# Five empty SyncE instructions behind the issue of SyncE's last store

## The chip, the cores and the metric

One core of a Trainium2 chip. The time is the device time of one execution in microseconds (us).

## The reference

A block of two branches on a 2048 x 640 bf16 input: a layer norm, a spectral filter (2-D real FFT, product with complex weights, inverse FFT) and a gated feed-forward network of width 1536.

```python
xn = _layernorm(x, axis=-1)
s = _A_ref(xn, A_w_r, A_w_i)                       # irfft2(rfft2(xn) * W)
g = _silu(_B_ref(xn, B_w_gate, B_w_up, B_w_down))  # (gelu(xn @ wg) * (xn @ wu)) @ wd
return x + s * g
```

## The kernel before

The kernel describes its work as tasks. A small planner of its own decides on which engine and in which order they run, and then every task emits its instructions. SyncE does nothing but wait and issue DMAs (its 211 records before: 134 issues, 73 semaphore checks, 4 drains); ScalarE issues the last piece of the last output tile.

```python
    def dma(out, in_, rank, size, after=(), new=(), use=(), slow=1.0, land=0):
        return add(lambda e: nc.sync.dma_start(...), "SP", (430, 430), rank, ...)   # cut
    ...
    if last and hi == D:
        add(lambda e: nc.scalar.dma_start(out=outv[:, n1, lo:], in_=res.tile[:, lo:]), "ACT", ...)
        return
    dma(lambda: outv[:, n1, lo:hi], lambda: res.tile[:, lo:hi], (0, 0, n1), ...)
    ...
    with tc.manual_schedule():
        for t in plan.run():
            t.emit(t.on)
    # leaving the tile context adds the closing sequence: SyncE makes nine checks of
    # semaphores, drains, and all five engines meet in a barrier
```

Of the kernel before, what the change touches and what calls it, by code (L numbers as in the profile page):

```python
# [222 lines left out]
def kernel(  # L223
# [11 lines left out]
    nc = tc.nc  # L235
# [778 lines left out]
    with tc.manual_schedule():  # L1014
        for t in plan.run():
            t.emit(t.on)


# [28 lines left out]
```

## Time and profile before

| | before |
|---|---|
| time, median of 3 runs | 202.47 us (202.35 to 202.68) |
| span of the profiled run | 200.7 us |
| TensorE busy | 195.5 us, 97% |
| last matmul to the end of the span | 196.74 to 200.72 us, 3.98 us |
| issue of SyncE's last store to the end | 197.61 to 200.72 us, **3.11 us** |

The last row I call *the stretch*.

L1042 is the closing line of the kernel (columns of its profile lines: engine, operation, count, shortest/median/longest duration in ns, first and last start).

```profile
L1042 SPq DRAIN  x2: 13/64/114, 199.4 to 199.8; - x2
```

Two drains follow one another on SyncE with nothing recorded between them. The first has ended at 199.459 us, the second starts at 199.849 us: a gap of 0.39 us, behind the last landing. I call it *the halt*; a *record* is one instruction as the trace lists it. The chain view does not show it either: its last step ends at 197.72 us, three us ahead of the end of the span.

### The profile page before, as it was taken

The numbers are of one execution on the slowest core, as the hardware profiler recorded it, in microseconds if no ns is written. First come the engines' busy times: TensorE is split into PE (matmuls) and PEld (weight loads), VectorE is DVE, ScalarE is ACT, GpSimd is POOL, SyncE is SP. The second block draws the span as 40 slices with busy tenths as digits, with TensorE's granted clock in tenths as the row PEclk, the third lists the DMA queues.
The fourth block names the chain that finished last, engine by engine and source line by source line (L and its number), as shares of the span: only waits on it lengthen the run. The fifth ranks groups of instructions, "written<-read, shape, count | busy, mean of one in ns | idle before, by whom it ended". The sixth has DMA issues, their size and how long they took to land.

```text
span 200.7 us, 4126 instructions
## 1 busy us (share of the span) xinstructions
PE 195.5 (97%) x1527; PEld 118.2 (59%) x1527; DVE 148.6 (74%) x318; ACT 128.3 (64%) x226; POOL 32.8 (16%) x71
## 2 busy tenths in 40 slices
PE   7999999999999999999999999999999999999992
PEld 3994444667544655777755455467765555457781
DVE  3689999996524159999998999933157788787773
ACT  3899989763722767767775767233466565776451
POOL 2414333896000000000000000000004122211210
PEclk9999999999999999999999999999999999999999
DMA  6999999896639976333244110116704242332432
GB/s 180 325 316 325 339 393 225 207 257 171 207 76 349 340 179 135 92 97 122 61 118 132 68 65 1 69 64 215 309 3 141 90 134 98 102 104 92 131 103 67
DMA packets 35895, 32.63 MB, mean 163 GB/s; under 512 B 10910, under 2 KB 32930, under 8 KB 35874
## 3 DMA queue, kind: packets, MB, share of 16 engines
q1 hardware_dynamic: 34434, 29.49, 50.4%
q0 software_dynamic: 1152, 2.66, 4.9%
q10 hardware_dynamic: 288, 0.20, 0.5%
q8 instruction: 12, 0.20, 0.4%
q14 instruction: 9, 0.07, 0.1%
HBM read 22.51 MB, written 9.19 MB: 158 GB/s over the span
## 4 chain that ended last, share of the span: by engine, by line
PE 97%; DVE 0%; ACT 0%; issue 0%; DVEq 0%
PE pg L886 26%; PE pu L886 26%; PE pg L976 13%; PE pu L976 13%; PE sp L697 3%; PE sp L830 3%; PE sp L772 2%; PE sp L806 2%; PE sp L368 2%; PE sp L670 2%; PE sp L532 2%; PE sp L690 1%; PE sp L824 1%; PE sp L463 1%; PE sp L478 1%; PE sp L653 0%
## 5 line engine op out<-in xcount | busy, mean ns | idle before, releaser
L886 PE MATMUL pu<-xnT,Wu 128*128 128x512 bf16 (+1 forms) x245 | 57.6, 366 | 0.0
L886 PE MATMUL pg<-xnT,Wg 128*128 128x512 bf16 (+1 forms) x245 | 57.5, 366 | 0.0
L907 DVE TENSOR_TENSOR uT<-pu,ge 128x512 bf16<-128x512 f32 x46 | 31.8, 690 | 20.6 <-PE pu L886 17.5
L976 PEld LDWEIGHTS <-uT 128*128 128x128 bf16 x396 | 37.9, 98 | 13.5
L903 ACT ACTIVATE ge<-pg 128x512 bf16<-128x512 f32 x46 | 27.6, 599 | 24.9 <-PE pg L886 24.4
L886 PEld LDWEIGHTS <-Wg 128*128 128x128 bf16 x285 | 25.5, 99 | 22.1
L886 PEld LDWEIGHTS <-Wu 128*128 128x128 bf16 x285 | 25.0, 98 | 21.6
L976 PE MATMUL pg<-Wd,uT 128*128 128x320 bf16 (+2 forms) x204 | 30.8, 293 | 0.0
L296 ACT CAST ma<-sp 128x644 bf16<-128x644 f32 (+1 forms) x32 | 23.4, 792 | 9.7 <-PE sp L830 7.9
L976 PE MATMUL pu<-Wd,uT 128*128 128x320 bf16 (+1 forms) x192 | 29.3, 297 | 0.0
L932 POOL COPY xr<-s 1x1 bf16<-1x1 bf16 x1 | 0.2, 179 | 100.3 <-DVE s L856 100.3
L933 POOL DMA_DIRECT2D xr<-in_A_x_dram x16 | 8.8, 550 | 32.3 <-DVE res L960 30.2
L296 ACT CAST IU<-sp 128x640 bf16<-128x640 f32 x16 | 10.9, 691 | 4.2 <-PE sp L772 4.1
L296 ACT CAST Vt<-sp 128x640 bf16<-128x640 f32 x16 | 10.8, 691 | 3.7 <-PE sp L806 3.7
L296 ACT CAST mc<-sp 128x640 bf16<-128x640 f32 x16 | 10.8, 700 | 3.4 <-DMA D<-mc 2.8
L985 ACT ACTIVATE th<-pu 128x320 f32<-128x320 f32 x15 | 6.6, 438 | 9.6 <-PE pu L976 9.3
L990 DVE SCALAR_TENSOR_TENSOR G<-th,pg 128x320 bf16<-128x320 f32 x15 | 7.2, 483 | 7.1 <-ACT th L985 6.9
L985 ACT ACTIVATE th<-pg 128x320 f32<-128x320 f32 x15 | 6.7, 445 | 7.8 <-PE pg L976 7.7
L990 DVE SCALAR_TENSOR_TENSOR G<-th,pu 128x320 bf16<-128x320 f32 x15 | 7.3, 484 | 4.6 <-ACT th L985 4.4
L433 POOL TENSOR_TENSOR RSTD<-MVA,mh 128x1 f32<-128x1 f32 x12 | 9.8, 815 | 4.0 <-DVE MVA L415 3.2
L848 DVE TENSOR_TENSOR mb<-ma 128x640 bf16<-128x640 bf16 x8 | 3.9, 491 | 6.8 <-ACT ma L296 6.8
L960 DVE TENSOR_TENSOR res<-yg,xr 128x640 bf16<-128x640 bf16 (+2 forms) x18 | 8.0, 449 | 0.2
(107 smaller groups left out, 255.1 us busy)
## 6 DMA issues: line engine op xcount, KB each, us to landing
BU<-D SPq DMA_DIRECT2D x8, 640.0 KB
D<-mc SPq DMA_DIRECT2D x8, 320.0 KB
D<-IU SPq DMA_DIRECT2D x8, 320.0 KB
xr<-in_A_x_dram POOLq DMA_DIRECT2D x16, 160.0 KB, 2.6
out_dram<-res SPq DMA_DIRECT2D x15, 160.0 KB
Wg<-in_B_w_gate_dram SPq DMA_DIRECT2D x6, 320.0 KB
Wu<-in_B_w_up_dram SPq DMA_DIRECT2D x6, 320.0 KB
Wd<-in_B_w_down_dram SPq DMA_DIRECT2D x6, 320.0 KB
```

The lines of the kernel that those rows point to most:

```text
L296: return nc.scalar.copy(out=out, in_=in_) if e == "ACT" else nc.vector.tensor_copy(out=out, in_=in_)
L433: nc.gpsimd.tensor_tensor(out=rstd, in0=var, in1=mh, op=ALU.pow)
L697: nc.tensor.matmul(into(q, ri), lhsT=sZ.tile[:, q, ri, :], rhs=FM[:, kinds[q][2] + (4 if ri and kind == 0 else 0), :], start=False, stop=T ...
L830: nc.tensor.matmul(into(q, s), lhsT=svs[s].tile[:, c, :], rhs=IM[:, q, :], start=False, stop=True, skip_group_check=True)
L886: nc.tensor.matmul(ps.tile[:, lo:hi + more], lhsT=w[:, c, t * P:(t + 1) * P], rhs=XR[:, c, lo + (lo > 0):hi + 1 if lo or more else hi] if ...
L903: nc.scalar.activation(out=ge.tile, in_=pg.tile if src is None else src, func=ACT.Gelu_apprx_tanh)
L907: nc.vector.tensor_tensor(out=u.tile, in0=pu.tile if src is None else src, in1=ge.tile, op=ALU.mult)
L933: nc.gpsimd.dma_start(out=sx.tile, in_=xv[:, n1, :])
L960: (nc.gpsimd if n1 in () else nc.vector).tensor_tensor(out=res.tile[:, lo:hi], in0=yg.tile[:, lo:hi], in1=sx.tile[:, lo:hi], op=ALU.add)
L976: nc.tensor.matmul(ps.tile[:, 0:hi - lo], lhsT=uT[grp, ks[i]].tile[:, j * P:(j + 1) * P], rhs=Wd[:, ks[i], lo:hi], start=(i == 0), stop=(i ...
L985: nc.scalar.activation(out=th.tile[:, 0:hi - lo], in_=ps.tile[:, 0:hi - lo], func=ACT.Tanh, scale=0.5)
L990: nc.vector.scalar_tensor_tensor(out=G2.tile[:, lo:hi], in0=th.tile[:, 0:hi - lo], scalar=1.0, in1=ps.tile[:, 0:hi - lo], op0=ALU.add, op1 ...
```

## The change

The intent is to place five instructions that do nothing on SyncE, behind its last store, and to keep the compiler from removing them.

```diff
     with tc.manual_schedule():
         for t in plan.run():
             t.emit(t.on)
+        for _ in range(5):
+            nc.sync.nop(nofuse=True)
```

## The prediction

The sum of the forecast is 202.47 + 0 = 202.47 us. The upper end of "all the ways above", 203.0 us, was that third rival: 202.47 us and, as an estimate, the 0.53 us that the last packet of queue q14 took in the trace of before (at 200.46 us).

> **What bounds the kernel now.** I read four views, in this order: the granted clock with the share table, the chain that ended last, the waits of SyncE's queue, and then the closing line of the kernel (the one that every engine shares at the end) cut into narrow windows.
>
> The page says first that the time is matrix time, and the chain says it again:
>
> ```profile
> span 200.7 us, 4126 instructions
> ## 1 busy us (share of the span) xinstructions
> PE 195.5 (97%) x1527; PEld 118.2 (59%) x1527; DVE 148.6 (74%) x318; ACT 128.3 (64%) x226; POOL 32.8 (16%) x71
> ...
> ## 4 chain that ended last, share of the span: by engine, by line
> PE 97%; DVE 0%; ACT 0%; issue 0%; DVEq 0%
> ```
>
> TensorE is busy for 195.5 of 200.7 us, and the chain that ended last is 97% TensorE. SyncE is on no step of it. A change that touches SyncE alone can therefore reach the end only in the few us behind the last matmul, where TensorE has nothing left. (The busy share alone is no proof that the array is at its peak, since matmul ends are modelled; here it only has to say who carries the chain.) The first number of the page I keep for later: 4126 instructions in the record.
>
> The end of the chain, from the window 190 to 202 us, shows where the compute stops:
>
> ```profile
> 196.07 0.69 PE pg L976 x12
> 196.76 0.02 issue
> 196.78 0.29 ACT G L996
> 197.07 0.02 issue
> 197.09 0.29 DVE yg L953
> 197.38 0.20 DVE res L960
> 197.59 0.13 DVEq L1042
> ```
>
> The columns are start, length, what. The last result is ready near 197.7 us, and the span ends at 200.7 us, so 3 us of it are stores, waits and the closing barrier. The timeline of the same stretch has the two last issues:
>
> ```profile
> 197.61 0.33 SPq L303 DMA_DIRECT2D out_dram<-res  x1
> 197.75 0.35 ACTq L965 DMA_DIRECT2D out_dram<-res  x1
> ```
>
> SyncE issues its last store at 197.61 us and is free at 197.94 us. ScalarE issues the very last store at 197.75 us. Behind its issue SyncE has nothing to do but the closing sequence, in which it checks one semaphore after another until all transfers have landed. Those checks, of SyncE alone, in the windows 197.9 to 198.42 us and 198.42 to 199.3 us:
>
> ```profile
> L1042 SPq EVENT_SEMAPHORE  x7: 28/28/28, 198.0 to 198.4; - x7
> ...
> L1042 SPq EVENT_SEMAPHORE  x1: 28/28/28, 199.2 to 199.2; - x1
> ```
>
> and the waits of SyncE's queue from 195 us on:
>
> ```profile
> SPq L303 <- DVE res L960: 3.3, 3, 1.9
> SPq L1042 <- DMA out_dram<-res: 0.8, 1, 0.8
> SPq L1042 <- PEq L1042: 0.7, 2, 0.5
> ```
>
> The trace has the first of the seven checks at 197.991 us and the seventh at 198.364 us: (198.364 - 197.991) / 6 = 62 ns from one sequencer-only instruction to the next, of which 28 ns are recorded as its duration. The eighth check runs only at 199.205 us: it waited for the landing of SyncE's own last store. The ninth, at 199.370 us, is let go by ScalarE's store. So SyncE is ready at 198.364 + 0.062 = 198.43 us and released at 199.205 us: **0.78 us of slack** right behind the place of the change. The view's 0.8 is this wait.
>
> [...]
>
> **The change, part by part.** It removes nothing and moves nothing on purpose. It asks for five empty instructions on SyncE, with no cycle count, no semaphore and no text, behind the last task of the plan. The plan is finished by then, so it cannot reorder anything.
>
> The first step is whether they exist at all. I built both kernels and compared the order of the instructions engine by engine. SyncE has 102 listed rows in each; the only difference on any engine is the line number of the closing line, L1042 before and L1044 after, because the file is two lines longer. I then counted every kind of instruction in the two built programs: 213 on SyncE in both, and no empty instruction in either. Last, the compiled instruction streams of the five engines are the same, byte for byte. The flag in the change only exempts an empty instruction from being fused; these five carry nothing that anyone waits for or that is printed, and they are dropped all the same before the program is written. "Must keep" is thus an intent that the build does not fulfil. **Cost of the change: 5 x 0 = 0 us.**
>
> The sum: 202.47 + 0 = 202.47 us.
>
> **The rivals.**
>
> *The five are kept on the chip after all* (the toolchain that builds for the chip differs from the one I looked at). Then SyncE runs five more sequencer-only instructions at 62 ns each, an estimate from the checks above: 5 x 62 = 310 ns, between 197.94 us and the first check. The seventh check moves from 198.364 to 198.67 us, still 0.78 - 0.31 = 0.47 us ahead of the landing at 199.205 us. The end does not move: 202.5 us. For it speaks only the wording of the change; against it stand the equal streams. What makes it harmless is that the store, not SyncE, sets the release.
>
> *The five are kept and not hidden.* If SyncE were held until the store had landed before the first of them, or the landing came earlier than the checks, the 310 ns would be added in full: 202.8 us, 0.15%. [...]
>
> [...]
>
> *The end is moved by something that is not the change.* The same instructions are loaded a second time, perhaps to other addresses or on another chip. The three runs of before lie between 202.35 and 202.68 us, 0.16% from end to end.
>
> **Range and chances.** All the ways above lie between 202.4 and 203.0 us, and the likeliest is an exact repeat. [...] I take 202.1 to 202.9 us as the range of 8 in 10. A difference of 2% would be 4 us, more than the whole 3 us behind the last result, and nothing here can make it: 0.99 for within 2%[...].
>
> **What would show it right or wrong.** In the record of the changed kernel: 4126 instructions again, not 4131; no empty instruction on SyncE between its last store and the first check, which starts some 45 ns after that store's issue has ended; seven checks at 62 ns, then the wait of about 0.8 us for the store; the same counts of the five engines and 97% TensorE in the chain. If 4131 stand there instead, my first step is wrong and the first rival is to be read off: the wait of the eighth check would shrink to about 0.5 us while the span stays. The prediction is wrong in its result if the eighth check comes later relative to the store's issue than 1.6 us (199.205 - 197.614), or if matmul time itself differs.

## The result

| | before | after |
|---|---|---|
| median | 202.41 us (4 runs, 202.29 to 202.68) | 202.49 us (4 runs, 202.28 to 202.66) |
| ratio | | 1.0001, 95% interval 0.9984 to 1.0019 |
| stretch | 3.109 us | 3.102 us |

Ratios are the mean time of one kernel's fast runs over the mean of the other's fast runs of the same rounds, so not quite the ratio of the medians. The time is the same.

The page after, its lines on span, busy time and chain:

```profile
span 200.6 us, 4108 instructions
## 1 busy us (share of the span) xinstructions
PE 194.4 (97%) x1509; PEld 117.7 (59%) x1527; DVE 148.7 (74%) x318; ACT 128.4 (64%) x226; POOL 33.0 (16%) x71
...
PE 96%; issue 1%; DVE 1%; ACT 0%; DVEq 0%
```

4108 instructions instead of the predicted 4126: the difference is in the matmuls alone, 1509 for 1527, while the weight loads, one to a matmul, are 1527 in both. Eighteen matmul records are missing from this trace; the other counts are equal. The total of such a page is therefore not fit to prove that nothing was added; the count of the engine in question is, and SyncE has 211 records in both.

The last two issues after, from the timeline, SyncE's checks in the windows 197.8 to 198.3 and 198.3 to 199.18 us, its two drains in the window 199.25 to 199.9 us, and the waits of SyncE's queue from 195 us on:

```profile
197.47 0.33 SPq L303 DMA_DIRECT2D out_dram<-res  x1
197.60 0.35 ACTq L965 DMA_DIRECT2D out_dram<-res  x1
...
L1044 SPq EVENT_SEMAPHORE  x7: 27/28/28, 197.8 to 198.2; - x7
...
L1044 SPq EVENT_SEMAPHORE  x1: 28/28/28, 199.1 to 199.1; - x1
...
L1044 SPq DRAIN  x2: 13/64/114, 199.3 to 199.7; - x2
...
SPq L1044 <- DMA out_dram<-res: 0.8, 1, 0.8
SPq L1044 <- PEq L1044: 0.7, 2, 0.5
```

The line number is two higher, and every instant is about 0.15 us earlier because the last matmul ended 0.15 us earlier. Apart from that it is the same tail: seven checks, the wait of 0.8 us, the check that is let go by the store, and the same gap between the drains. No empty instruction is in it.

### The profile page after: what moved, and what is told of

Same layout as the page of the kernel before. It is cut to its first block, busy times and chain, and to the rows that moved or that the text cites. A ratio compares the mean times of both kernels' runs of the same rounds, so it can differ in the third digit from the quotient of the medians.

```text
span 200.6 us, 4108 instructions
## 1 busy us (share of the span) xinstructions
PE 194.4 (97%) x1509; PEld 117.7 (59%) x1527; DVE 148.7 (74%) x318; ACT 128.4 (64%) x226; POOL 33.0 (16%) x71
## 3 DMA queue, kind: packets, MB, share of 16 engines
q0 software_dynamic: 1152, 2.66, 5.3%
## 4 chain that ended last, share of the span: by engine, by line
PE 96%; issue 1%; DVE 1%; ACT 0%; DVEq 0%
PE pu L886 26%; PE pg L886 25%; PE pg L976 13%; PE pu L976 13%; PE sp L697 3%; PE sp L830 3%; PE sp L772 2%; PE sp L806 2%; PE sp L368 2%; PE sp L670 2%; PE sp L532 2%; PE sp L690 1%; PE sp L824 1%; PE sp L463 1%; PE sp L478 1%
## 5 line engine op out<-in xcount | busy, mean ns | idle before, releaser
L886 PE MATMUL pg<-xnT,Wg 128*128 128x512 bf16 (+1 forms) x234 | 56.3, 365 | 0.5
L418 ACT ACTIVATE th<-X 128x640 bf16<-128x640 bf16 x11 | 8.1, 745 | 0.0
```

The source lines that it names most:

```text
L418: nc.scalar.activation(out=place(junk, (D,)), in_=x, func=ACT.Copy, scale=-1.0 / D, accum_out=less)
L886: nc.tensor.matmul(ps.tile[:, lo:hi + more], lhsT=w[:, c, t * P:(t + 1) * P], rhs=XR[:, c, lo + (lo > 0):hi + 1 if lo or more else hi] if ...
```

## The experiments

All outputs are right. Three questions: are the five really gone on the chip, what would five have cost that are kept, and what the kept ones do instead.

To keep an empty instruction it is enough to give it a text, `hint="empty"`; the build then writes it into SyncE's stream, which has 215 instructions as compiled before and 220 with five. The runs text1 to text400 differ from the change only in this and in the count:

```diff
-        for _ in range(5):
-            nc.sync.nop(nofuse=True)
+        for _ in range(N):
+            nc.sync.nop(hint="empty", nofuse=True)
```

### bare400: four hundred without a text

```diff
-        for _ in range(5):
+        for _ in range(400):
             nc.sync.nop(nofuse=True)
```

> Four hundred of the change's empty instructions in the place of five. Theory (the build drops them): ratio 1.000 within 0.003, time 202.4 us, 211 instructions of SyncE in the record, no gap between SyncE's last store and its first check beyond some 45 ns. Rival (they are kept and cost 62 ns each, hidden up to 0.78 us): 400 x 62 ns - 0.78 us = 24.0 us more, 226.4 us.

202.25 us (4 runs), ratio 0.9997 (0.9983 to 1.0012); stretch 3.098 us; 211 records of SyncE. Its seven checks in the window 197.7 to 198.2 us start 46 ns after the store's issue has ended:

```profile
L1044 SPq EVENT_SEMAPHORE  x7: 27/28/28, 197.8 to 198.1; - x7
```

Four hundred are gone as five are. The first step of the prediction is shown on the chip.

### text5, text20, text40: five, twenty and forty that are kept

> Five empty instructions that carry a short text, so that the build keeps them (220 instead of 215 instructions in SyncE's compiled stream). Theory (kept, but hidden in 0.78 us of slack): ratio 1.000 within 0.003; in the record the first check starts about 0.31 us later after the last store's issue (5 x 62 ns), the eighth check's wait shrinks from 0.8 to about 0.5 us, and the stretch from the issue of SyncE's last store to the end of the span stays 3.06 us. Rival (not hidden, or held until the store has landed): that stretch grows by 0.31 us to 3.37 us.

> Twenty kept ones. Theory: 20 x 62 ns = 1.24 us against 0.78 us of slack, so the stretch from the issue of SyncE's last store to the end grows by about 0.46 us to 3.5 us, and the 0.8 us wait is gone; the ninth check, which waits for ScalarE's store, absorbs up to about 0.1 us of that. Ratio about 1.002. [...] Rival (held until the landing): stretch 4.3 us.

> Forty kept ones. Theory: 40 x 62 ns = 2.48 us, less 0.78 us of slack = 1.70 us more: stretch 4.76 us, time 204.1 us, ratio 1.0084. [...] Rival (held until the landing): 2.48 us more in full, ratio 1.012.

| | time, ratio (95% interval) | first check after the store's issue has ended | stretch |
|---|---|---|---|
| text5 | 202.19 us, 0.9991 (0.9977 to 1.0004) | 0.27 us | 2.65 us |
| text20 | 202.45 us, 1.0001 (0.9983 to 1.0020) | 1.27 us | 2.99 us |
| text40 | 203.05 us, 1.0033 (1.0018 to 1.0047) | 1.99 us | 3.70 us |

The runs of before in these rounds have a median of 202.33 us (9 runs).

None of the three stretches is what any theory said (and the 3.06 us that the expectations start from should have been the 3.11 us of the table). Two things were wrong. First, an empty instruction cost less than a check: in text400 below they start 37 ns apart, against the 62 ns of the checks before. Second, and unforeseen by all theories, five of them make the stretch **0.46 us shorter**. What went is the gap between the drains. In text5, the empties, the checks in the windows 197.85 to 198.2 and 198.2 to 199.05 us, and the two drains in the window 199.07 to 199.2 us:

```profile
L1018 SPq NOP  x5: 13/13/18, 197.6 to 197.8; - x5
...
L1044 SPq EVENT_SEMAPHORE  x5: 28/28/28, 197.9 to 198.2; - x5
...
L1044 SPq EVENT_SEMAPHORE  x4: 28/28/28, 198.6 to 199.0; - x4
...
L1044 SPq DRAIN  x2: 7/10/13, 199.1 to 199.2; - x2
```

The drains are now 75 ns apart from start to start (403 before), and the second lasts 7 ns (114 before). In their place there is a gap among the checks: the fifth starts at 198.152 us, the sixth at 198.564 us, though neither has anything new to wait for. The same gap, in text20, stands between the tenth and the eleventh empty instruction, which wait for nothing at all (windows 198.2 to 198.9 and 198.9 to 199.6 us):

```profile
L1018 SPq NOP  x10: 13/13/18, 198.3 to 198.7; - x10
...
L1018 SPq NOP  x10: 13/13/18, 199.1 to 199.5; - x10
```

Counted through SyncE's records from the start of the program, the halt stands ahead of the 208th in each of before, after, bare400, text5, text20 and text40, and is 0.38 to 0.39 us long. So it belongs to a place in the instruction stream and not to an instruction. Before, the 208th is the second closing drain. With five more ahead of it, it is the sixth check, which runs while SyncE waits for its store anyway. No wait of the profile names this halt: the two waits on PEq stand in text5 just as before (two, 0.7 us in all), and they are the closing barrier.

The sum for text40 closes with this. The first check comes 1.99 us after the end of the issue instead of 0.045 us, in which the halt is contained; the nine checks then run without a wait and the ninth starts at 2.479 us instead of 1.424 us, 1.055 us later; and from the ninth check to the end it is 0.46 us shorter, because the halt is no longer there. 1.055 - 0.46 = 0.59 us, which is 3.70 - 3.11.

### text1, text2, text3: how many it takes

> What the first four runs left: five kept empty instructions made the stretch from the issue of SyncE's last store to the end shorter, 2.65 us against 3.11 us before, and in all of these records SyncE halts for 0.39 us just ahead of its 208th recorded instruction, whatever that is (the second closing drain before, a check with five, an empty instruction with twenty and forty). Theory P (a place in the instruction stream costs 0.39 us; each kept instruction moves it one instruction earlier in the sequence): with three, the 208th is the eighth check, which waits for the store in any case, so the halt is fully hidden: stretch 2.65 us, 0.46 us less than before, ratio 0.9978. Rival E (the empties themselves help, each some 0.09 us): 3.11 - 3 x 0.09 = 2.84 us. Rival N (chance): 3.11 us.

> One kept. Theory P: the 208th is the first closing drain, which stands behind the last landing, so the 0.39 us stay in the chain: halt ahead of that drain, stretch 3.0 to 3.1 us. Rival E: 3.02 us, and the halt stays ahead of the second drain or goes.

> Two kept. Theory P: the 208th is the ninth check, which waits only 0.14 us beyond the eighth, so 0.39 - 0.14 = 0.25 us stay in the chain: stretch about 2.65 + 0.25 = 2.90 us. Rival E: 2.93 us; the two are told apart by text1 and text3, not here, but the halt must stand ahead of the ninth check.

| | the 208th record of SyncE | stretch | expected of the place in the stream |
|---|---|---|---|
| before | second drain | 3.11 us | |
| text1 | first drain | 3.12 us | 3.0 to 3.1 us |
| text2 | ninth check | 2.95 us | 2.90 us |
| text3 | eighth check | 2.65 us | 2.65 us |

The closing line of text1 and text2 in the window 198.9 to 200 us, then of text3 (windows 199.2 to 200.5 us):

```profile
L1044 SPq EVENT_SEMAPHORE  x2: 28/28/28, 199.1 to 199.3; - x2
L1044 SPq DRAIN  x2: 7/64/121, 199.7 to 199.8; - x2
```

```profile
L1044 SPq EVENT_SEMAPHORE  x3: 17/28/28, 199.2 to 200.0; - x3
L1044 SPq DRAIN  x2: 7/22/36, 199.7 to 199.8; - x2
```

```profile
L1044 SPq EVENT_SEMAPHORE  x7: 28/28/28, 199.2 to 200.3; - x7
L1044 SPq DRAIN  x2: 7/10/13, 200.4 to 200.5; - x2
```

text1 and text2 come 0.02 and 0.05 us above what the place in the stream said. With one, the halt moves from between the drains to ahead of both (the last check ends at 199.3 us, the drain comes at 199.7 us) and gains nothing: it is still behind the last landing. With two it stands ahead of the ninth check, and part of it lies under the 0.14 us which that check waits for ScalarE's store. With three it stands ahead of the eighth check and is gone in the wait of 0.8 us. It can't be seen there, because that check waits anyway; a packet of 8192 bytes, of the queue shown under text400, points to the place: it starts 1.06 us after the seventh check does, and 1.02 to 1.32 us after the record ahead of the halt in the other runs. The rival, a gain of 0.09 us for each empty instruction, said 3.02, 2.93 and 2.84 us; one gains nothing, and three gain all that five do. text2 alone could not have told the two apart.

In time, text3 is 202.18 us (6 runs) against 202.46 us (11 runs of before), ratio 0.9985 (0.9962 to 1.0008). Its profiled run is one of the long ones (span 201.2 us, matmuls to 197.69 us), with the short stretch all the same.

### mid5: five kept, eight stores earlier

```diff
     with tc.manual_schedule():
-        for t in plan.run():
+        order = plan.run()
+        far = [t for t in order if t.on == "SP"][-9]
+        for t in order:
             t.emit(t.on)
-        for _ in range(5):
-            nc.sync.nop(nofuse=True)
+            if t is far:
+                for _ in range(5):
+                    nc.sync.nop(hint="empty", nofuse=True)
```

> The five kept ones not behind the last store but eight stores earlier, where SyncE waits for results anyway. Theory P: only the count of instructions ahead matters, so the halt falls ahead of a check inside the wait just as with five behind the last store, and there is nothing between the last issue and the first check: stretch 2.65 us, ratio 0.9978, the first check 45 ns after the issue has ended. Rival (what helps is the pause between the last store and the checks): stretch 3.11 us, ratio 1.000.

The empties are at 179 us, some 18 us ahead of the last store; then the checks in the windows 197.6 to 198.0 and 198.0 to 199.0 us:

```profile
L1021 SPq NOP  x5: 13/13/18, 178.9 to 179.0; - x5
...
L1047 SPq EVENT_SEMAPHORE  x5: 28/28/28, 197.7 to 197.9; - x5
...
L1047 SPq EVENT_SEMAPHORE  x3: 28/28/28, 198.4 to 198.9; - x3
```

Five checks, the halt of 0.385 us, and the sixth at 198.4 us as in text5; the first check comes 54 ns after the issue has ended, so there is no pause behind the store. Stretch 2.66 us; 202.33 us (6 runs), ratio 0.9989 (0.9968 to 1.0010). It is the count of instructions ahead that matters, not a pause at the end.

### text400: is it once, or every so often?

> Four hundred kept ones behind SyncE's last store. [...] Rival O (a single event, such as something that happens once per program): one halt, ahead of the 208th. The cost of an empty one is 35 to 40 ns as in the record with forty: stretch about 3.7 + 360 x 0.0375 = 17.2 us, and 17.6 us with the second halt; time about 216.5 us.

217.12 us. It was run on another chip. The theory that is cut had two halts, the rival one. Neither number was right: there are four, ahead of the 208th, the 336th, the 464th and the 592nd record of SyncE. The empties in the windows 197.7 to 198.25, 198.4 to 203.5, 203.5 to 208.5, 208.5 to 213.5 and 213.5 to 215 us:

```profile
L1018 SPq NOP  x10: 13/13/18, 197.8 to 198.2; - x10
...
L1018 SPq NOP  x128: 13/13/18, 198.6 to 203.3; - x128
...
L1018 SPq NOP  x128: 13/13/14, 203.6 to 208.3; - x128
...
L1018 SPq NOP  x128: 13/13/14, 208.7 to 213.3; - x128
...
L1018 SPq NOP  x6: 13/13/14, 213.7 to 213.9; - x6
```

10 + 3 x 128 + 6 = 400. Within a group the empties start 37 ns apart ((208.323 - 203.643) us / 127); across a halt the next one comes 392, 348, 342 and 357 ns after the one before. The DMA part of the page over the window 198 to 215 us shows what goes with it; GB/s is in 40 slices of 0.425 us:

```profile
GB/s 104 128 19 0 0 0 0 0 0 0 0 0 0 0 19 0 0 0 0 0 0 0 0 0 0 0 19 0 0 0 0 0 0 0 0 0 0 0 19 0
...
q14 instruction: 4, 0.03, 0.6%
```

Four packets of q14, a queue that the page calls "instruction", one for each halt: 19 GB/s x 0.425 us is 8 KB. In the trace each has 8192 bytes and starts 0.62 to 0.65 us after the first instruction behind a halt. So in this run a halt came every 128 records of SyncE, three times, and one such packet with each halt. The kernel before agrees: its 80th record, 128 ahead of the 208th, starts 0.467 us after the 79th has ended (0.03 to 0.06 us in the ten records ahead of it), and 1.1 us later an 8192-byte packet of q14 follows; as that record is a check, a wait may be part of it. What SyncE does during a halt, and why the spacing is 128, was not shown.

The stretch was 17.93 us, against 17.2 to 17.6 us expected.

### text4: the time of the version without the exposed halt

> Four kept ones, a repeat of the version with the halt inside the wait. Theory P: the halt stands ahead of the seventh check, at the 208th again, hidden: stretch 2.65 us, and the time 0.2 to 0.5 us under that of before, ratio 0.9978. Rival: the lower times with three, five and five in the middle (0.27 to 0.30 us under their own runs of before, each within its interval) were scatter: ratio 1.000.

202.18 us (6 runs, 201.77 to 202.58) against 202.66 us (11 runs, 202.35 to 203.17): ratio **0.9977 (0.9962 to 0.9992)**. They were run on another chip. The halt stands ahead of the seventh check (windows 197.85 to 198.3 and 198.3 to 199.12 us), and the stretch is 2.66 us:

```profile
L1044 SPq EVENT_SEMAPHORE  x6: 28/28/28, 197.9 to 198.2; - x6
...
L1044 SPq EVENT_SEMAPHORE  x3: 28/28/28, 198.7 to 199.1; - x3
```

The means of text3, text5 and mid5 are 0.28, 0.28 and 0.29 us under those of their own runs of before, each with an interval that contains 1; this one lies 0.58 us under and its interval does not. All four have the short stretch, 0.45 us below that of before. Taken together by a plain pooled estimate, each within its own rounds (23 runs against 31 of before), they are 0.38 us faster, with a 95% interval of about 0.20 to 0.56 us, which agrees with the 0.45 us of the stretch. So a gain of about 0.2% is shown, for the four together better than for any one of them.

## Why the prediction was right

**The five cost nothing because they do not exist.** Right, and shown: no record of them after, and four hundred of them change nothing either. The time, 202.49 us, lies within 0.02 us of the 202.47 us predicted; that it is so close is luck, since runs of one kernel lie several tenths of a us apart.

**The check after.** Seven checks, the wait of 0.8 us, 211 records of SyncE: right. The total of 4126 records was a poor witness: 4108 stood there, for eighteen missing matmul records. The chain reads 96% TensorE and 1% issue where 97% was forecast; with matmul records missing, this says nothing about the change.

**The rival of five that are kept.** It did not come about, so it did not touch the result, but it was wrong in three ways. An empty instruction takes 37 to 53 ns from start to start in text5, where I had taken the 62 ns of a check. The wait of the eighth check does not shrink to about 0.5 us but to 0.2 us, as the halt moves in front of it. And the end does not stay: it comes 0.46 us earlier. The step that failed there is "the end does not move", which rested on the slack ahead of the release alone.

**The third rival.** It made SyncE's tail longer by up to 0.53 us and was set aside with next to nothing because the streams are equal; for the change as built that held (stretch 3.102 us against 3.109 us). What it missed was in the tail already before the change: the 0.39 us between the drains, in a closing line that I read only to the ninth check. The direction was the opposite of the one it gave: with five kept instructions the halt moves away, and the end comes 0.46 us earlier instead of 0.53 us later.

**Empty instructions that wait for the store.** They did not: in text5 they run from 197.6 to 197.8 us, long before the landing that lets the eighth check go at 198.8 us.

## What to carry to other kernels

Compare the built instruction streams before reasoning about the cost of a source change: a flag against fusion is no promise that an instruction is kept (none of the 400 in bare400 was), and a program that is byte for byte the same has no cost to estimate. Where a tail consists of checks and drains, read the gaps between starts through to the last one, since the halt of 0.39 us here appeared in no list of waits. It fell behind the last landing, and three to five kept instructions moved it into a wait, which was worth 0.45 us; each one more or less moved it by one instruction (text1 to text5), so a later change in the number of SyncE's instructions may move it again. Judge such small effects by the stretch behind the last matmul and not by the time, which scattered by 0.35 to 1.3 us over the runs of one kernel.
